# The first chunk of sequence 0 fetched on two hardware queues and cast on two engines, instead of one casting fetch on GpSimd's queue

## The chip, the cores and the metric

The kernel runs on one core of one Trainium2 chip. The metric is the device time of one execution in microseconds. Three timed runs of the kernel before gave 863.15, 863.33 and 863.42 us; the median is 863.33 us.

The core has a matrix engine (TensorE, "PE" in the profile, with "PEld" for its weight loads), VectorE ("DVE"), ScalarE ("ACT"), GpSimd ("POOL") and SyncE ("SP"), which here only issues transfers. Transfers are issued from three queues: GpSimd's (the profile's "software_dynamic" queue q0), SyncE's (hardware queue q1) and ScalarE's (hardware queue q10). All three feed the same 16 DMA engines.

## The reference, cut to what matters

```python
X = rfft(x, axis=1)                       # x: 8 sequences of 3008 rows of 256, fp32
y = irfft(X * (filt_r + 1j * filt_i)[None], n=3008, axis=1)
t = y.reshape(24064, 256)
xn = t / sqrt(mean(t * t, -1) + 1e-6) * rms_g
g, val = xn @ w_gate, xn @ w_val          # 256 -> 1536
out = (g * sigmoid(g) * val) @ w_out      # 1536 -> 256
```

A global filter mixes each sequence along its length, and a gated feed-forward block follows on all 24064 rows.

## The kernel before, in words

The transform of length 3008 = 47 x 64 is done as matmuls: a 64-point stage with the table `wa`, a 47-point stage with the tables `wb`, the filter, and the two stages back with `wi` and `wai`. Everything on TensorE is fp16 with fp32 accumulation, apart from a few fp32 transposes. The feed-forward block (`gv`, `down`) is the bulk of the work: 8 sequences x 6 tiles x 12 slices of the hidden size.

The mixing of sequences 1 to 7 is spread between the feed-forward slices of the sequences before them by a planner (`fit`, `at`), and the order of each engine's instructions is then fixed. Sequence 0 has nothing to hide behind: its mixing is a preface, written out by hand ahead of the main loop, in this order on TensorE:

- `fill(10)` (L643): ten matmuls of 512 columns on a zeroed tile whose result nobody reads; they need no transfer.
- `a0(0)` (L644), then `fill(4)`, `a0(1, 2)`, three small transposes (`psg`, L650 and L651), `fill(3)`, `a0(3)`, `fill(4)`, `a0(4, 5)`. One `a0(gq)` is two `a0_unit` calls (L353): eight matmuls of 128 columns in all (L357), which take four of the 24 columns of x as weights and `wa` as the moving operand; ScalarE and VectorE copy the two banks out (L195, L197).
- `f_unit` (L385, matmuls L389), which transposes the filter, alternating with `tr0_unit` (L362, transposes L367), then `b_unit`, `yt0_unit`, `bi_unit`, `first_norm` and the first `gv`.

x of one sequence comes in four chunks of six columns (`XC` = 6, `NXC` = 4). `x_load` (L174) fetches one with a single casting transfer on GpSimd's queue, fp32 in memory to fp16 in a tile of the pool `xp` (4 buffers). `a0(0)` reads columns 0 to 3, all in chunk 0; `a0(1)` reads 4 to 7, `a0(2)` 8 to 11, `a0(3)` 12 to 15, and `a0(4, 5)` 16 to 23, so that the last two need chunk 3.

On GpSimd's queue stand, in order: chunks 0 to 3 of x (L614, L186), the filter in six pieces of 512 KB (`f_load`, L382) with a part of `wb` before the sixth, the rest of `wb`, `wi`, and the feed-forward weights (`w_load`, L594). A transfer of this queue takes one of eight semaphores in turn, and the ninth waits until the first has landed, the tenth until the second, and so on; GpSimd's waits in its timeline show this. On SyncE's queue stand `tab` (L616: `wa`, `wai` and the identities, 160 KB) and three transfers of at most 1 KB into `tail` (L619, L620), which the transposes `psg` read.

The fp32 staging pool `stg` has four buffers, used in turn: the three pairs of filter pieces, then the feed-forward weights, then the tiles `y`.

The start of the preface, as it stands in the kernel before:

Of the kernel before, what the change touches and what calls it, by code (L numbers as in the profile page):

```python
# [10 lines left out]
FP32 = mybir.dt.float32  # L11
FP16 = mybir.dt.float16
# [5 lines left out]
N1 = 47  # L18
N2 = 64
NF = N // 2 + 1  # L20
P = 128
D = 256
# [3 lines left out]
H = 24  # L26
# [7 lines left out]
XC = 6  # L34
NXC = H // XC
# [66 lines left out]
def kernel(  # L102
# [11 lines left out]
    nc = tc.nc  # L114

    tab_np, wb_np, wi_np = _make_tables()
    tab_d = nc.inline_tensor(tab_np, name="tab_t").ap()
# [6 lines left out]
    stg = ctx.enter_context(tc.tile_pool(name="stg", bufs=4))  # L124
    xp = ctx.enter_context(tc.tile_pool(name="xp", bufs=4))
# [17 lines left out]
    tab = glob.tile([P, 5 * P], FP16)  # L143
# [20 lines left out]
    st = {b: {"x": {}, "t1": {}, "t2": {}, "s": {}, "yt": {}, "t4": {}, "y": {}, "sq": {},  # L164
              "u": {}, "xn": {}} for b in range(B)}

    def raw(src, row, ap):
        return bass.AP(tensor=src.tensor, offset=src.offset + row * D, ap=ap)
# [5 lines left out]
    def x_load(b, c):  # L174
        t = xp.tile([P, XC, D], FP16, tag="xc", name="xc")
        row = b * N + c * XC
        src = lambda n, w, lo=0: raw(x.flatten_outer_dims(), row + lo, [[N1 * D, n], [H * D, 2], [1, w * D]])
        if b == B - 1 and c == NXC - 1:
            w = XC - 1
            nc.vector.memset(t[96:P, w, :], 0.0)  # L180
            nc.gpsimd.dma_start(t[:, 0:w, :].rearrange("p a d -> p (a d)"), src(N2, w))
            nc.gpsimd.dma_start(t[0:P - 2, w, :], src(N2 - 1, 1, w))
            nc.gpsimd.dma_start(t[P - 2:P - 1, w, :],
                                raw(x.flatten_outer_dims(), row + w + (N2 - 1) * N1, [[D, 1], [1, D]]))
        else:
            nc.gpsimd.dma_start(t.rearrange("p a d -> p (a d)"), src(N2, XC))  # L186
        st[b]["x"][c] = t

    def bank(i, name):
        pool, tag = ((psM, "mx"), (psG, "pg"), (psV, "pv"), (psB, "mb"), (psO, "po0"))[i]  # L190
        return pool.tile([P, 512], FP32, tag=tag, name=name)

    def copy(eng, out, in_, scale=None):
        if eng == "A":
            nc.scalar.activation(out=out, in_=in_, func=AXT.Copy, **({} if scale is None else {"scale": scale}))  # L195
        elif scale is None:
            nc.vector.tensor_copy(out=out, in_=in_)  # L197
        else:
            nc.vector.tensor_scalar(out=out, in0=in_, scalar1=scale, scalar2=None, op0=ALU.mult)
# [223 lines left out]
    def fill(n, bk=0):  # L423
        ps = bank(bk, "pf")
        for _ in range(n):
            nc.tensor.matmul(ps, ss3[0][:, 0, 0, :], ss3[0].rearrange("p k e q -> p (k e q)")[:, 0:512], start=True, stop=True)
# [181 lines left out]
                                        op0=ALU.mult, op1=ALU.mult)  # L608

    with tc.manual_schedule():  # L610
        nc.vector.memset(ss3[0], 0.0)
        nc.vector.memset(epsb, 1e-6 * Y_SCALE * Y_SCALE)
        nc.scalar.activation(out=warm, in_=epsb.to_broadcast([P, 4]), func=AXT.Sqrt)
        for c in range(NXC):  # L614
            x_load(0, c)
        nc.sync.dma_start(tab, tab_d)  # L616
        tail = op.tile([P, 4, D], FP32, tag="o3", name="tail")
        for f, src in ((0, filt_i), (1, filt_r)):
            nc.sync.dma_start(tail[0:1, f, :], raw(src, NF - 1, [[D, 1], [1, D]]))  # L619
# [18 lines left out]
        def a0(*gqs):  # L638
            for gq in gqs:
                for dh in range(2):  # L640
                    a0_unit(gq, dh, E[dh], 1 + dh)

        fill(10)  # L643
        a0(0)  # L644
        fill(4)
        a0(1, 2)
# [32 lines left out]
        for p in range(UN + 3):  # L679
            if 3 <= p < UN:  # L680
                b_unit(0, od[p], (0, 3)[p % 2])
                s_part(0, od[p], 1)
            if p == 0:
                f_unit(2, 1, 1, "A")
                f_neg(4, 12, (1,))
                f_last()
                f_neg(0, 4)
                w_load(2)
                wo_load(0)
                f_neg(16, 16)  # L690
                wo_load(1)
                for c in range(3):
                    x_load(1, c)
                for q in range(3):
                    w_gain(q)
            if 2 <= p < UN + 1:
                yt0_unit(od[p - 2], "A", 1)
            if p == UN + 1:
                yt0_unit(UN - 1, "V", 1, slice(0, 2))
                yt0_unit(UN - 1, "A", 0, slice(2, 4))  # L700
            if 4 <= p < UN + 3:
                bi_unit(0, od[p - 4], "AV"[p == UN + 1], 2)
            if UN + 1 <= p < UN + 3:
                fill(1, 1)
# [8 lines left out]
        nc.gpsimd.tensor_copy(out=seen, in_=st[0]["t4"][1][:, 0, 0:4])  # L713
        wo_load(2)
        x_load(1, 3)
        first_norm()

# [92 lines left out]
        for b in range(1, B):  # L810
            t = (b - 1) * 72
# [73 lines left out]
```

## Time and profile before

| | |
|---|---|
| time, median of three runs | 863.33 us (863.15 to 863.42) |
| profiled execution, span from first to last instruction | 861.4 us |
| PE busy | 852.4 us, 99% of the span |
| ACT, DVE, POOL busy | 612.4, 557.2, 297.8 us |
| PE's share of the chain that ended last | 96% |
| first matmul of `a0(0)` | 6.06 us after the span's start |
| first matmul of `f_unit` | 13.03 us |

For the profiled execution the profile gives the span; the median of the timed runs is 1.9 us above it, and this part lies ahead of the first and behind the last instruction. PE is busy nearly all the time, and its busy time includes the matmuls of `fill`, which do no work of the reference. All that the change touches lies in the first 14 us, so the views to read are those of that stretch: the chain of waits, the timeline of PE, ACT and POOL, and the DMA packets of each queue in narrow windows. In a timeline, a row gives start, duration, engine, line, operation and count; the bracket at its end is the idle time just before it and what ended it. In a DMA window, a queue's row gives packets, MB, and the time that the packets took as a share of 16 engines.

### The profile page before, as it was taken

The numbers are of one execution on the slowest core, as the hardware profiler recorded it, in microseconds if no ns is written. First come the engines' busy times: TensorE is split into PE (matmuls) and PEld (weight loads), VectorE is DVE, ScalarE is ACT, GpSimd is POOL, SyncE is SP. The second block draws the span as 40 slices with busy tenths as digits, with TensorE's granted clock in tenths as the row PEclk, the third lists the DMA queues.
The fourth block names the chain that finished last, engine by engine and source line by source line (L and its number), as shares of the span: only waits on it lengthen the run. The fifth ranks groups of instructions, "written<-read, shape, count | busy, mean of one in ns | idle before, by whom it ended". The sixth has DMA issues, their size and how long they took to land.

```text
span 861.4 us, 17024 instructions
## 1 busy us (share of the span) xinstructions
PE 852.4 (99%) x6142; PEld 532.2 (62%) x6142; DVE 557.2 (65%) x926; ACT 612.4 (71%) x1339; POOL 297.8 (35%) x346
## 2 busy tenths in 40 slices
PE   8999999999999999999999999999999999999997
PEld 6755666566666666666666666666666666665664
DVE  5857655776666666666666676767666665555554
ACT  4986777787588756887577856888567765777443
POOL 5725742453144322534034430444123430132000
PEclk9999999999999999999999999999999999999999
DMA  9995778765975476656755548433564331521101
GB/s 283 270 204 124 150 164 168 139 130 121 197 137 129 121 150 111 151 107 147 139 127 113 132 98 180 108 87 101 131 127 93 97 70 42 124 54 49 62 25 50
DMA packets 198237, 107.98 MB, mean 125 GB/s; under 512 B 158566, under 2 KB 182520, under 8 KB 198152
## 3 DMA queue, kind: packets, MB, share of 16 engines
q1 hardware_dynamic: 189464, 85.52, 44.1%
q0 software_dynamic: 8544, 21.24, 12.7%
q8 instruction: 48, 0.79, 0.4%
q14 instruction: 37, 0.30, 0.1%
q10 hardware_dynamic: 144, 0.13, 0.0%
HBM read 45.78 MB, written 35.65 MB: 95 GB/s over the span
## 4 chain that ended last, share of the span: by engine, by line
PE 96%; DMA 1%; ACT 1%; DVE 1%; issue 0%; POOL 0%; POOLq 0%
PE po L563 28%; PE pg L546 28%; PE pv L546 28%; PE psb L241 3%; PE psi L285 3%; PE psn L314 2%; PE psa L206 2%; DMA fs<-in_filt_i_dram 1%; PE psy L418 1%; PE psf L389 1%; PE pst L367 0%; ACT sg L550 0%; POOL xc L186 0%; DVE s L231 0%; DVE hh L551 0%
## 5 line engine op out<-in xcount | busy, mean ns | idle before, releaser
L551 DVE TENSOR_TENSOR hh<-pv,sg 128x512 f16<-128x512 f32 (+2 forms) x578 | 391.5, 678 | 286.4 <-ACT sg L550 221.9
L550 ACT ACTIVATE sg<-pg 128x512 f16<-128x512 f32 (+2 forms) x578 | 337.4, 584 | 217.6 <-PE pg L546 213.4
L546 PE MATMUL pg<-xn,wg 128*128 128x512 f16 (+2 forms) x1156 | 338.1, 374 | 0.1
L546 PE MATMUL pv<-xn,wv 128*128 128x512 f16 (+2 forms) x1156 | 338.1, 374 | 0.0
L563 PE MATMUL po<-wo,hh 128*128 128x256 f16 x2256 | 332.7, 273 | 0.0
L563 PEld LDWEIGHTS <-hh 128*128 128x128 f16 x2256 | 213.4, 98 | 105.5 <-issue 0.6
L268 POOL TENSOR_TENSOR ss<-s,s 128x384 f16<-128x384 f16 x112 | 101.9, 911 | 273.2 <-DVE s L234 245.2
L546 PEld LDWEIGHTS <-wv 128*128 128x128 f16 x1156 | 112.9, 98 | 130.7
L546 PEld LDWEIGHTS <-wg 128*128 128x128 f16 x1156 | 111.4, 98 | 17.0 <-issue 0.3
L340 POOL TENSOR_TENSOR xt<-y,rho 128x1024 f16<-128x1024 f32 (+1 forms) x46 | 85.4, 1856 | 2.8
L322 ACT ACTIVATE junk<-y 128x256 f16<-128x256 f32 x180 | 74.3, 413 | 2.8
L231 DVE TENSOR_TENSOR s<-psb,ff 128x384 f16<-128x384 f32 x124 | 67.6, 547 | 0.7 <-ACT ff L195 0.6
L234 DVE TENSOR_TENSOR s<-psb,ff 128x384 f16<-128x384 f32 x124 | 67.6, 546 | 0.0
L195 ACT ACTIVATE uu<-psi 128x384 f16<-128x384 f32 (+1 forms) x127 | 61.6, 486 | 1.5 <-DMA out_dram<-o 0.5
L195 ACT ACTIVATE y<-psn 128x512 f32<-128x512 f32 (+1 forms) x95 | 55.7, 588 | 4.2
L285 PEld LDWEIGHTS <-yt 96*128 96x128 f16 x512 | 35.4, 97 | 26.7 <-issue 1.0
L332 POOL TENSOR_TENSOR rho<-u,mhalf 128x4 f32<-128x4 f32 (+1 forms) x46 | 46.5, 1010 | 3.8
L330 POOL TENSOR_SCALAR u<-ss 128x4 f32<-128x4 f32 (+1 forms) x46 | 8.9, 193 | 104.8 <-ACT junk L322 103.8
L195 ACT ACTIVATE t<-psa 128x512 f16<-128x512 f32 x70 | 41.4, 594 | 3.1 <-PE psa L206 1.7
L285 PE MATMUL psi<-wi,yt 96*128 96x96 f16 x512 | 42.9, 205 | 0.1
L241 PE MATMUL psb<-wb,t 96*128 96x96 f16 x480 | 40.1, 206 | 0.3 <-DVE s L234 0.2
L241 PEld LDWEIGHTS <-t 96*128 96x128 f16 x480 | 28.7, 97 | 12.8 <-DVE s L234 3.3
(101 smaller groups left out, 366.2 us busy)
## 6 DMA issues: line engine op xcount, KB each, us to landing
out_dram<-o SPq DMA_DIRECT2D x40, 512.0 KB, 3.6
xc<-in_x_dram POOLq DMA_DIRECT2D x31, 384.0 KB, 5.6
z_tmp<-t SPq DMA_DIRECT2D x28, 384.0 KB, 2.7
t<-z_tmp SPq DMA_DIRECT2D x28, 384.0 KB, 6.0
out_dram<-o SPq DMA_DIRECT2D x7, 384.0 KB, 2.7
fs<-in_filt_i_dram POOLq DMA_DIRECT2D x3, 512.0 KB, 10.8
fs<-in_filt_r_dram POOLq DMA_DIRECT2D x3, 512.0 KB, 11.2
ws<-in_moe_w_gate_dram POOLq DMA_DIRECT2D x3, 512.0 KB, 9.8
```

What stands on the lines that cost most here:

```text
L195: nc.scalar.activation(out=out, in_=in_, func=AXT.Copy, **({} if scale is None else {"scale": scale}))
L231: eng.tensor_tensor(out=o, in0=ps, in1=f1, op=ALU.mult)
L234: eng.tensor_tensor(out=o, in0=ps[:, :, ::-1, :], in1=f2, op=ALU.mult)
L241: nc.tensor.matmul(ps[:, ts(k, KR)], st[b]["t2"][kk // KC][:, kk % KC, ds(dh * P, P)], wb[0:KR, kk, :], start=True, stop=True)
L268: nc.gpsimd.tensor_tensor(out=ss3[g % 3][:, :, dh, 0:KR], in0=s[0], in1=s[1], op=ALU.add)
L285: nc.tensor.matmul(ps[:, k, :], yt[0:KR, k, dh, :], wi[0:KR, 4 * g + k, :], start=True, stop=True)
L322: nc.scalar.activation(out=junk, in_=y[:, i, ts(u, D)], func=AXT.Square, accum_out=ss[:, 2 * i + u:2 * i + u + 1])
L340: nc.gpsimd.tensor_tensor(out=xt[:, 0:n, :], in0=y.rearrange("p a (u d) -> p (a u) d", u=2)[:, 0:n, :], in1=rho[:, 0:n].unsqueeze(2).to_br ...
L546: nc.tensor.matmul(ps[:, 0:w], wt[:, dt_, ts(jt, P)], xn[:, q0:q1, dt_, :], start=(dt_ == 0), stop=(dt_ == 1))
L550: nc.scalar.activation(out=sg[:, c], in_=pg[:, 0:w], func=AXT.Silu)
L551: nc.vector.tensor_tensor(out=hh[:, c], in0=pv[:, 0:w], in1=sg[:, c], op=ALU.mult)
L563: nc.tensor.matmul(po[s4 // 2][:, s4 % 2, :], hh[:, ts(s4, P)], wo[:, jt, :], start=(jt == 0 and s4 % 2 == 0), stop=(jt == JT - 1 and (s4 ...
```

## The change

Chunk 0 of sequence 0 is no longer fetched by `x_load`. A new function fetches it as fp32, without a cast, into a buffer of the staging pool: columns 2 to 5 (512 KB) on ScalarE's queue, columns 0 and 1 (256 KB) on SyncE's queue. The transfer of `tab` is moved ahead of it, to the top, and stays the first on SyncE's queue; the transfers into `tail` follow behind columns 0 and 1. On ScalarE the issue stands ahead of the activation that loads the first table. GpSimd's queue begins with chunk 1. Ahead of `a0(0)`, ScalarE casts columns 0 and 1 and VectorE columns 2 to 5 into the fp16 tile that the matmuls read. `fill(10)` becomes `fill(7)`. Nothing is changed behind `a0(0)`; on every engine the order of the other instructions is the same.

```diff
+    X0 = 2
+
+    def x_first():
+        t = xp.tile([P, XC, D], FP16, tag="xc", name="xc")
+        raw_t = stg.tile([P, XC, D], FP32, tag="stg", name="xs")
+        for eng, lo, hi in ((nc.scalar, X0, XC), (nc.sync, 0, X0)):
+            eng.dma_start(raw_t[:, lo:hi, :].rearrange("p a d -> p (a d)"),
+                          raw(x.flatten_outer_dims(), lo, [[N1 * D, N2], [H * D, 2], [1, (hi - lo) * D]]))
+        st[0]["x"][0] = t
+        return t, raw_t
...
     with tc.manual_schedule():
+        nc.sync.dma_start(tab, tab_d)
+        xt0, xs0 = x_first()
         nc.vector.memset(ss3[0], 0.0)
         nc.vector.memset(epsb, 1e-6 * Y_SCALE * Y_SCALE)
         nc.scalar.activation(out=warm, in_=epsb.to_broadcast([P, 4]), func=AXT.Sqrt)
-        for c in range(NXC):
+        for c in range(1, NXC):
             x_load(0, c)
-        nc.sync.dma_start(tab, tab_d)
         tail = op.tile([P, 4, D], FP32, tag="o3", name="tail")
...
-        fill(10)
+        fill(7)
+        copy("A", xt0[:, 0:X0, :], xs0[:, 0:X0, :])
+        copy("V", xt0[:, X0:XC, :], xs0[:, X0:XC, :])
         a0(0)
         fill(4)
```

## The prediction

> **What bounds the kernel now.** I read the chain of waits first. The page gives PE 96% of it, so a change to the start moves the end by as much as it moves the moment from which PE runs without a gap. The chain over the first 15 us shows that moment:
>
> ```profile
> 0.63 0.63 issue
> 1.25 2.37 POOL xc L186 x4
> 3.63 9.27 DMA fs<-in_filt_i_dram
> 12.90 0.14 issue
> 13.03 1.06 PE psf L389 x8
> ```
>
> Until 13.03 us the chain is GpSimd's queue: four chunks of x, then the first filter piece, which lands at 12.90. From 13.03 to the first feed-forward matmul at 43.4 the chain has only PE, ACT and DVE pieces. So the first filter matmul is the milestone: what moves it moves the end one for one, and an earlier landing helps only if PE can use it. The timeline of PE shows how far it is from being late itself:
>
> ```profile
> 1.45 4.45 PE L426 MATMUL pf<-ss 128*128 128x512 f16 x10 [1.45 <-DVE epsb L612]
> 6.06 1.03 PE L357 MATMUL psa<-tab,xc 128*128 128x128 f16 x8 [0.17 <-DMA xc<-in_x_dram]
> 6.89 1.14 PE L426 MATMUL pf<-ss 128*128 128x512 f16 x4
> 7.86 1.06 PE L357 MATMUL psa<-tab,xc 128*128 128x128 f16 x16
> ...
> 11.22 0.28 PE L357 MATMUL psa<-tab,xc 128*128 128x128 f16 x2
> 11.68 0.96 PE L357 MATMUL psa<-tab,xc 128*128 128x128 f16 x14 [0.18 <-DMA xc<-in_x_dram]
> 13.03 0.74 PE L389 MATMUL psf<-tab,fs 128*128 128x128 f32 x5 [0.40 <-DMA fs<-in_filt_i_dram]
> ```
>
> Two things stand in it. Between 6.06 and 13.03 PE is nearly full: it waits for chunk 3 for some 0.35 us (11.33 to 11.68) and for the filter for 0.5. PE may thus start a0(0) at most 0.9 us later before it becomes the bound. And PE runs at half rate at first: the ten fills take 0.43 us each, the eight matmuls from 6.06 take 0.83/8 = 0.104 us, while the 16 from 7.86 to 8.75 take 0.056 each and later fills 0.216. The rate doubled about 7.1 us in, 5.6 us after the first matmul. (The granted clock reads 1.00 in these windows; I take the spacing.)
>
> **What the change removes.** GpSimd's queue loses chunk 0. Its timeline gives chunk landings from the waits that they end: 6.30, 8.16, 10.07, 11.91, so 1.85 us of transfer per chunk, and 1.28 us per filter piece (13.18 to 14.46). The 0.52 us of issue that goes hides nothing. The ninth transfer, which waited for chunk 0, now goes out at once; the others wait for the same transfers as before. Three fills go: 1.28 us of PE work that covered waiting, so nothing on the path; their cover for the half rate is costed below.
>
> **What it adds on the queues.** The two hardware pieces are 512 KB (one filter piece: 1.28 us of all 16 engines) and 256 KB (half: 0.64), so the data is 1.92 us instead of 1.85. The gain can only be in when it flows. tab was issued at 0.73 and its packets ran from 1.72 to 2.6; GpSimd's first transfer was issued at 1.25 and its packets began at 2.75. So the hardware pieces have about 1.0 us of free engines, of which tab needs 0.64 (its share of 1.7 to 2.7). After that they meet chunk 1. How the engines divide themselves decides the case. Two windows show it:
>
> ```profile
> q0 software_dynamic: 14, 0.04, 87.1%
> ```
>
> This is 2.85 to 3.60 us: the first software packets hold the engines for most of 0.75 us, and no hardware packet moves, though tail transfers issued up to 1.88 us are still due (five hardware packets follow in 3.6 to 4.3). And 51.5 to 54.3 us, a z_tmp store of 128 packets of 3072 B on SyncE's queue beside GpSimd's:
>
> ```profile
> q0 software_dynamic: 127, 0.34, 61.4%
> q1 hardware_dynamic: 133, 0.38, 36.7%
> ```
>
> The two queues go one packet for one. The store's packets needed 0.367 x 2.8 = 1.03 us of the engines and took 2.8. Per engine a store has 8 packets, and so have tab, each hardware piece and each chunk.
>
> So per engine: a software packet is 1.85/8 = 0.23 us, a 4 KB one 0.16, a 2 KB one 0.08, a tab one 0.055. By 2.75, less a start of 0.2, some four tab packets and four of ScalarE's piece are done. Then 0.85 us of the first software packet, to 3.6; four rounds of tab, ScalarE's piece and software, 4 x (0.055 + 0.16 + 0.23) = 1.8, to 5.4; then SyncE's piece, queued behind tab, eight rounds of (0.08 + 0.23) = 2.5, to 7.9. With 0.1 for the landing, columns 0 and 1 are there at 8.0. Lower bound: hardware first, tab + 1.92 = 2.56 us from 1.72, and the 0.3 us by which tab landed after its last packet: 4.6. Upper: completion packets take turns too, 0.5 more: 8.5. I take 8.0, since both rows show alternation.
>
> For GpSimd's queue, chunk 1 takes chunk 0's place behind the same first packet, with 1.7 us of hardware work left in its way: chunk 3 and the filter land only 0.2 to 0.4 us earlier (with hardware first, up to 1.2).
>
> **The casts.** ScalarE's (512 elements): between 0.41 (256 elements with a sum, L322) and 0.60 (512 elements); I take 0.59, plus 0.1 of hand-over, on the path. VectorE's (1024 elements): 0.69 (1024 fp16, L197) to 1.2 (twice the 512-element 0.69, less one start); its data comes at 5.5, so it ends by 6.8, under ScalarE's. If SyncE's piece came first, VectorE's would set the time, 0.1 to 0.6 more. Behind the waiting casts only the copies of a0 are queued, which need them anyway. The issue ahead of ScalarE's table load (0.36 to 0.66 us) delays a load that ended at 2.0 and that nobody needs before the cast. The tail transfers behind SyncE's piece are used 2.8 us after a0(0) starts: hidden. The staging buffer must be free before a weight transfer at 15.7: hidden. So a0(0) starts at 8.0 + 0.7 = 8.7 instead of 6.06.
>
> **PE from there.** The chain in PE's order from a0(0) to the last of a0(5) at full rate: 0.45 + 0.86 + 0.89 + 0.50 + 0.65 + 0.45 + 0.86 + 0.89 = 5.55 us (windows of PE's timeline; before: 6.06 to 12.47 with 0.35 of waiting and 0.5 of half rate). At half rate each stretch doubles. Seven fills end at 1.45 + 7 x 0.43 = 4.45, and PE then stands for over 4 us. Bounds for the half rate behind a0(0): none (the rate is kept through the gap), to 6.8 us. The one row is 5.6 us from a first matmul with one 0.35 us pause; I take 4, since the weight of it is unknown, which costs 2.0. The first filter matmul then comes at 8.7 + 5.55 + 2.0 + 0.05 = 16.3 instead of 13.03: 3.3 us later. By then the filter has long landed. Nothing gives the time back: from there the chain has no DMA piece. **The sum** is 863.33 + 3.3 = 866.6 us; made against the profiled execution it is a span of 861.4 + 3.3 = 864.7, with the same 1.9 around it.
>
> Two rules of the Trainium skill are weighed here. The Trainium skill, TensorE: Matmul & The Clock Gate, "What's actually happening", says that the array is at half clock until one fixed window of about 3.4 us was busy, and again after an idle one; the 5.6 us here agree. By it seven fills (3.0 us) are too short, the half rate would last an estimated 2.5 to 6 us behind a0(0), and the sum would be 866 to 868.
> The Trainium skill, DMA: Bandwidth & Descriptors, "Queues, rings and completion order", says that an engine drains a packet of some 9 to 17 descriptors from one queue before it turns to the next; the 127 against 133 above do not show that. By it the eight descriptors of a piece would go in one turn, which is the second rival.
>
> **Rivals.**
> 1. Late data, but the half rate ends soon or the alternation is milder: a0(0) at 7.0 to 7.5, half rate for 1 to 3 us: milestone at 13.1 to 14.6, 863.4 to 864.9. For it: the 0.85 us of the first software packet need not repeat behind hardware traffic. Against: no hardware packet between 2.85 and 3.60.
> 2. The other side: a hardware piece goes through in one turn. Then columns 0 and 1 land at 4.6 to 5.0, VectorE's cast ends by 5.6, PE stands for about 1 us, its half rate ends within some 2 us, and its chain would be done at 5.6 + 5.55 + 1.0 = 12.15, so the filter decides: 0.6 to 1.2 us earlier, 862.4. It decides if a0(0) starts before 6.5. For it: idle engines before 2.75 and between 2.85 and 3.6. Against: the 127 and 133.
> 3. More than 0.2% faster would need the filter to land 1.7 us earlier; the engines are busy 0.99 and more from 4.0 us on, so all of the idle time before would have to be filled.
>
> **How the numbers follow.** 0.2% of 863.33 is 1.73 us, about what a measurement can tell from no change. Forecast (a0(0) after 7.8, half rate again): 0.62, range 864.9 to 868.0. Rival 1: 0.18, of which 0.03 is above 865.06. Rival 2: 0.16. Rival 3: 0.04. So slower 0.65, same 0.31, faster 0.04. For 8 in 10 the range is 862.8 to 867.9: it takes in most of rival 2 and drops the ends.
>
> **What would show it.** Right: a0(0) waits until 8 to 9 us and is released by ScalarE's cast, which waits for SyncE's piece; fills behind a0(0) at 0.43 us; the first filter matmul at 15 to 17.5 with no DMA wait; all later stages shifted by the same amount. Wrong: hardware packets in one burst before 4.5 us, fills at 0.216 us right behind a0(0), or a filter matmul that still waits for its transfer.

## The result and the profile after

The changed kernel takes 867.15 us (median of four runs, 866.71 to 868.0) against 863.24 us for the kernel before (four runs, 863.15 to 863.42): a ratio of 1.0046 with a 95% interval of 1.0032 to 1.006. It is slower by 3.9 us. The forecast was 866.6, slower by 3.3.

The profiled execution of the changed kernel took 867.2 us, with a span of 865.4 against 861.4. The first lines of its page:

```profile
span 865.4 us, 17023 instructions
PE 852.3 (98%) x6139; PEld 532.8 (62%) x6139; DVE 558.5 (65%) x927; ACT 613.1 (71%) x1340; POOL 297.5 (34%) x345
```

PE's busy time is what it was (852.4 before), since the three fills that are gone are made up for by matmuls that run longer at half rate. The span is 4.05 us longer (865.43 against 861.38), and by so much more PE stands. The chain of waits over the first 18 us shows most of it (start, duration, what):

```profile
0.73 0.35 SPq L622
1.09 0.06 issue
1.15 7.19 DMA xs<-in_x_dram
8.34 0.02 issue
8.36 0.64 ACT xc L206
9.00 0.05 issue
9.04 1.03 PE psa L368 x8
...
15.64 0.89 PE psa L368 x16
16.53 0.02 issue
16.55 1.14 PE psf L400 x8
```

The chain that ran through GpSimd's queue and the filter now runs through SyncE's piece of chunk 0, issued at 1.15 and landed 7.19 us later, then ScalarE's cast, then PE alone. The first filter matmul comes at 16.55 instead of 13.03. The timeline of PE has the rate at which it went there:

```profile
1.45 3.17 PE L437 MATMUL pf<-ss 128*128 128x512 f16 x7 [1.45 <-DVE epsb L625]
9.04 1.03 PE L368 MATMUL psa<-tab,xc 128*128 128x128 f16 x8 [4.42 <-ACT xc L206]
9.87 1.91 PE L437 MATMUL pf<-ss 128*128 128x512 f16 x4
11.58 1.60 PE L368 MATMUL psa<-tab,xc 128*128 128x128 f16 x16
...
14.61 1.03 PE L437 MATMUL pf<-ss 128*128 128x512 f16 x4
15.47 1.06 PE L368 MATMUL psa<-tab,xc 128*128 128x128 f16 x16
16.55 1.14 PE L400 MATMUL psf<-tab,fs 128*128 128x128 f32 x8
```

The seven fills stand 0.43 us apart to their end, so PE has not reached its full rate when they are over; then it stands for 4.42 us. The four fills behind `a0(0)` take 1.91 us, the four from 14.61 take 1.03: by their starts 0.43 us each against 0.216. The rate doubles within the 16 matmuls from 11.58, at about 12.7, so the half rate lasted 3.7 us behind `a0(0)`. No bracket names a DMA from 9.04 on. From there nothing is given back: the first gate matmul of the feed-forward block moves from 43.38 to 46.93, and all 578 gate activations from 44 us to the end stand 3.55 to 3.56 us later than in the trace of before.

One part of the difference does not lie at the start. The last store of each kernel, in SyncE's timeline, of before:

```profile
857.64 0.56 SPq L578 DMA_DIRECT2D out_dram<-o  x1
```

and of after:

```profile
861.23 0.54 SPq L589 DMA_DIRECT2D out_dram<-o  x1
```

From its start to the end of the span are 861.38 - 857.64 = 3.74 us before and 865.43 - 861.23 = 4.20 us after. So 0.46 us are lost behind the last store, which the change doesn't touch. The last store itself is 861.23 - 857.64 = 3.59 us later, nearly all of it from the start (3.52 at the first filter matmul), and 3.59 + 0.46 make the 4.05 by which the span grew.

GpSimd's waits show that its own queue, relieved of chunk 0, became later and not earlier:

```profile
8.79 0.55 POOL L635 DMA_DIRECT2D wb<-wb_t  x1 [2.50 <-DMA xc<-in_x_dram]
10.50 0.53 POOL L393 DMA_DIRECT2D fs<-in_filt_r_dram  x1 [1.16 <-DMA xc<-in_x_dram]
12.34 0.54 POOL L637 DMA_DIRECT2D wb<-wb_t  x1 [1.31 <-DMA xc<-in_x_dram]
13.64 0.54 POOL L638 DMA_DIRECT2D wb<-wb_t  x1 [0.76 <-DMA fs<-in_filt_i_dram]
```

These end with the landings of chunks 1, 2, 3 and the first filter piece; before, the same waits ended at 8.16, 10.07, 11.91 and 13.18. The queue is 0.4 to 0.6 us late throughout, without a consequence, since PE reaches the filter only at 16.55.

The DMA packets of each queue (packets, MB, share of 16 engines) from 2.75 to 4.25 us:

```profile
q10 hardware_dynamic: 107, 0.39, 71.6%
q1 hardware_dynamic: 27, 0.06, 10.8%
```

and from 5.5 to 8.0 us:

```profile
q0 software_dynamic: 173, 0.49, 101.2%
q1 hardware_dynamic: 29, 0.04, 4.7%
```

In the first there is no packet of GpSimd's queue (q0) at all, although its first transfer was issued at 1.26 and the engines were 18% idle. ScalarE's piece landed at 5.42. Of SyncE's, 111 of the 128 packets had started by 5.5 as well; 17 are among the 29 of the second window, the rest there being `tail`'s and a few of 4 B. But these 17 run beside GpSimd's queue, the last starts at 7.7, and a transfer has landed when its last packet has. The trace has 16 completion records of this piece, read here as one for each engine: thirteen stand by 6.06, the last three at 6.94, 7.86 and 8.34. So a few engines make the piece late.

### The profile page after: what moved, and what is told of

Read it like the earlier page. It is cut to its first block, busy times and chain, and to the rows that moved or that the text cites. A ratio compares the mean times of both kernels' runs of the same rounds, so it can differ in the third digit from the quotient of the medians.

```text
span 865.4 us, 17023 instructions
## 1 busy us (share of the span) xinstructions
PE 852.3 (98%) x6139; PEld 532.8 (62%) x6139; DVE 558.5 (65%) x927; ACT 613.1 (71%) x1340; POOL 297.5 (34%) x345
## 4 chain that ended last, share of the span: by engine, by line
PE 96%; ACT 1%; DVE 1%; DMA 1%; issue 0%; SPq 0%
PE po L574 28%; PE pg L557 28%; PE pv L557 28%; PE psb L252 3%; PE psi L296 2%; PE psn L325 2%; PE psa L217 2%; DMA xs<-in_x_dram 1%; PE psy L429 1%; PE psf L400 1%; PE pf L437 0%; PE psa L368 0%; PE pst L378 0%; DVE s L242 0%; DVE hh L562 0%
```

## The experiments

Each is made on the changed kernel unless it says otherwise, and its ratio is to the kernel before on the same chip, whose medians were 863.16 to 863.37 us. A hardware transfer is one on SyncE's or ScalarE's queue. What the forecast rested on comes first: the half rate, then the landing, then the queue of GpSimd, and last the part at the end that no step had foreseen.

### The half rate of PE

**Sixteen fills instead of seven**, so that PE works until shortly before the data:

```diff
-        fill(7)
+        fill(16)
```

> The changed kernel with 16 fills ahead of a0(0) instead of 7, nothing else. They last from 1.45 to at most 1.45 + 16 x 0.43 = 8.3 us, less if the rate doubles on the way, so they end before columns 0 and 1 are there (cast ended at 9.0). Theory (the seven fills leave PE standing for 4.4 us, and the half rate of the 3.66 us behind a0(0) costs half of that): a0(0) still at about 9.0, the fills behind it at 0.216 us, the first filter matmul at 14.7 instead of 16.55, time 867.15 - 1.85 = 865.3 us. Rival (the late data is all of it, the rate comes back by itself): filter matmul at 16.5, 867.1 us.

Measured: 865.39 us (eight runs, 863.47 to 865.73), ratio 1.0023 (1.0013 to 1.0034). The timeline of PE in this kernel:

```profile
1.45 6.31 PE L437 MATMUL pf<-ss 128*128 128x512 f16 x16 [1.45 <-DVE epsb L625]
9.12 0.62 PE L368 MATMUL psa<-tab,xc 128*128 128x128 f16 x8 [1.37 <-ACT xc L206]
9.58 1.03 PE L437 MATMUL pf<-ss 128*128 128x512 f16 x4
...
14.88 1.14 PE L400 MATMUL psf<-tab,fs 128*128 128x128 f32 x8
```

The data comes no earlier (`a0(0)` at 9.12), yet the fills behind it run at 0.216 us and the first filter matmul comes at 14.88. From `a0(0)` to it are 5.76 us, against 7.51 in the changed kernel: the half rate is worth 1.75 us, shown by taking it away alone. Here the rate had doubled at about 6.9 us, within the sixteen fills, and a pause of 1.37 us did not bring the half rate back. In the changed kernel it had not doubled before the pause, so that kernel does not show what its 4.42 us of standing do by themselves: seven fills are too few to reach the full rate.

**The kernel before with seven fills**, the smallest part of the change done alone:

```diff
-        fill(10)
+        fill(7)
```

> The kernel before with 7 fills instead of 10, nothing else: chunk 0 comes on GpSimd's queue as before. Theory (half rate after a pause): a0(0) stays at 6.06, PE stands from 4.6 to 6.06, the half rate then lasts 2.5 to 6 us behind a0(0), PE's chain ends at 6.06 + 5.6 + 1.3 to 3.0 = 13.0 to 14.7, so the filter matmul comes 0 to 1.6 us later: 863.2 to 864.9 us, and more scatter between executions than before. Rival (the number of fills is indifferent as long as the data is the bound): 863.2 us, filter matmul at 13.03.

Measured: 864.09 us (ten runs, 863.34 to 864.34), ratio 1.0009 (1.0 to 1.0019). Chunk 0 comes on GpSimd's queue as before, 0.25 us later in the profiled execution. Its timeline of PE:

```profile
6.31 1.03 PE L357 MATMUL psa<-tab,xc 128*128 128x128 f16 x8 [1.69 <-DMA xc<-in_x_dram]
7.14 1.91 PE L426 MATMUL pf<-ss 128*128 128x512 f16 x4
...
14.13 1.15 PE L389 MATMUL psf<-tab,fs 128*128 128x128 f32 x8
```

With a pause of only 1.69 us, `a0(0)` and the fills behind it run at half rate as in the changed kernel, and the first filter matmul comes 1.1 us late, of which 0.25 is the landing. So dropping three fills costs some 0.9 us even with no late data. The sum had called the fills "nothing on the path" but for the half rate, which is what shows here.

### The landing of SyncE's piece

**GpSimd's queue held back until chunk 0 is there**, by two tiny copies on GpSimd that read both pieces ahead of its first transfer:

```diff
+        for c in (0, X0):
+            nc.gpsimd.tensor_copy(out=seen, in_=xs0[:, c, 0:4])
         for c in range(1, NXC):
             x_load(0, c)
```

> The changed kernel with two small copies on GpSimd ahead of chunk 1, which read chunk 0's two hardware pieces, so that no software transfer is under way while they land. Theory (SyncE's piece was late because it shared the engines with GpSimd's queue): it lands at about 4.8 us instead of 8.34, VectorE's cast and ScalarE's end by 5.9, a0(0) at about 5.9. Rival (it is late by its own place: behind tab on SyncE's queue, 2 KB packets, beside ScalarE's piece): it lands at 7 to 8 us still. Either way GpSimd's queue begins 4 us later, the first filter piece lands at about 15 to 17 us and is then the bound: 865.5 to 867.5 us.

Measured: 867.43 us (one run). Its DMA issues (columns: size, us from issue to landing) and the timeline of ACT and PE:

```profile
xs<-in_x_dram SPq DMA_DIRECT2D x1, 256.0 KB, 4.2
```

```profile
5.42 0.63 ACT L206 ACTIVATE xc<-xs 128x512 f16<-128x512 f32 x1 [2.50 <-DMA xs<-in_x_dram]
6.11 1.03 PE L368 MATMUL psa<-tab,xc 128*128 128x128 f16 x8 [1.49 <-ACT xc L206]
...
10.77 0.96 PE L368 MATMUL psa<-tab,xc 128*128 128x128 f16 x14 [1.71 <-DMA xc<-in_x_dram]
...
13.79 1.91 PE L437 MATMUL pf<-ss 128*128 128x512 f16 x4
```

Without GpSimd's packets SyncE's piece lands at 5.40 instead of 8.34. So 2.9 us of its 7.19 are what GpSimd's queue costs it; the theory is right, its 4.8 was too early by 0.6. The kernel gains nothing, since GpSimd's first issue then stands at 6.09, chunk 1 lands at 10.72, and some 1.7 us after the wait for it PE falls back from full rate to half rate (four fills in 1.91 us at 13.79). This is one execution.

**One transfer for all six columns on ScalarE's queue**, first with seven fills, then with ten:

```diff
-        for eng, lo, hi in ((nc.scalar, X0, XC), (nc.sync, 0, X0)):
+        for eng, lo, hi in ((nc.scalar, 0, XC),):
```

> The changed kernel with all six columns of chunk 0 in one transfer of 768 KB on ScalarE's queue; the casts are unchanged. ScalarE's piece of 512 KB landed at 5.42 us with packets at about 0.16 us each per engine. Theory (SyncE's piece is late because it stood second on its queue, so that on some engines it met software packets one for one): one transfer that starts at 2.0 lands at 6.0 to 6.7, a0(0) at 6.8 to 7.5, filter matmul at 14.0 to 15.0 (half rate as in the changed kernel), 864.7 to 865.6 us. Rival (any 768 KB of hardware transfer ends on the same slow engine at about 8.3): a0(0) at 9.0, 867.1 us.

> All of chunk 0 in one transfer on ScalarE's queue, as in the run before it, with 10 fills instead of 7. There a0(0) came at 6.24 us, the rate doubled at 9.0, the filter piece landed at 12.74 and PE's chain ended at 13.33. Theory (what was left of the loss is the half rate behind seven fills): the fills end at 5.73, PE pauses half a microsecond, the rate doubles at 5 to 8.3, PE's chain would end by 12.1 to 13.0, so the filter's landing decides: first filter matmul at 12.9, 863.17 - 0.15 = 863.0 us, within 0.1% of the kernel before, and little scatter. Rival (a cost of the new fetch that is not seen yet): 863.6 us, as with seven fills.

Measured: 863.63 us with seven fills (ten runs, 862.44 to 864.02; ratio 1.0002, 0.9993 to 1.0012), and 862.78 with ten (eleven runs, 862.31 to 863.14; ratio 0.9994, 0.9985 to 1.0003). With seven, the 768 KB are issued at 0.73 and land at 5.54, earlier than all that was expected: three times the data of SyncE's piece, on one hardware queue, is there 2.8 us before it. With ten fills the timeline of PE has

```profile
12.55 1.06 PE L400 MATMUL psf<-tab,fs 128*128 128x128 f32 x8 [0.39 <-DMA fs<-in_filt_i_dram]
```

and the filter is the bound again, landed at 12.42 instead of 12.90. This is the lowest median of all, 0.4 us under the kernel before, which eleven runs can't tell from no change.

**Both pieces on ScalarE's queue**, to see if SyncE's queue is to blame:

```diff
-        for eng, lo, hi in ((nc.scalar, X0, XC), (nc.sync, 0, X0)):
+        for eng, lo, hi in ((nc.scalar, X0, XC), (nc.scalar, 0, X0)):
```

> The changed kernel with both pieces on ScalarE's queue, still as two transfers, columns 2 to 5 first; tab alone on SyncE's; 7 fills. Tells whether two transfers or the second queue made columns 0 and 1 late. Theory (it is the second piece that meets software packets one for one on an engine that is behind, on whichever queue it stands): the second piece lands at 6.5 to 8.3, a0(0) at 7.2 to 9.0, 865 to 867 us. Rival (SyncE's queue, behind tab and sharing turns with ScalarE's, made it late): as with one transfer on ScalarE's queue, lands at 5.6, a0(0) at 6.3, 863.7 us.

Measured: 868.56 us (four runs, 868.06 to 868.85), ratio 1.006 (1.0046 to 1.0073), the slowest of all. Its DMA issues:

```profile
xs<-in_x_dram ACTq DMA_DIRECT2D x1, 512.0 KB, 4.2
...
xs<-in_x_dram ACTq DMA_DIRECT2D x1, 256.0 KB, 7.7
```

Issued at 0.73 and 1.40, they land at 4.94 and 9.14. So neither SyncE's queue nor the transfer of `tab` ahead is needed to make a piece late. As in the changed kernel, though, the late piece is the second transfer of its queue.

**Halves by partition**, 64 partitions each, so that both pieces have 64 packets of 6144 B and equal size:

```diff
-        for eng, lo, hi in ((nc.scalar, X0, XC), (nc.sync, 0, X0)):
-            eng.dma_start(raw_t[:, lo:hi, :]...,
+        for eng, h in ((nc.scalar, 0), (nc.sync, 1)):
+            eng.dma_start(raw_t[h * 64:h * 64 + 64]...,
```

> The changed kernel with chunk 0 split by partitions instead of columns: partitions 0 to 63 (384 KB, packets of 6144 B) on ScalarE's queue, 64 to 127 on SyncE's queue behind tab; same bytes, same two queues, 7 fills. In the changed kernel each engine has 8 packets of 4096 B and 8 of 2048 B, here 8 of 6144 B in all, as in the single transfer that landed at 5.54. Theory (what counts is how many hardware packets still wait on the slowest engine when the software packets come, as each then waits for one of them): both halves land at 5.5 to 6.0 us, a0(0) at 6.3 to 6.8, 863.6 to 864.5 us. Rival (two hardware transfers on two queues make an engine late whatever the packets): the later half lands at about 8.3, 867 us.

Measured: 867.63 us (four runs, 867.13 to 868.24), ratio 1.005 (1.0034 to 1.0067). ScalarE's half, issued at 0.73, lands at 5.23; SyncE's, issued at 1.15, at 7.66, against 5.5 to 6.0 expected. So the number of packets alone doesn't set it; again the piece issued second is the late one. `a0(0)` starts at 8.43, 0.6 us earlier than in the changed kernel, and the time is no shorter: the half rate lasts longer here, and from `a0(0)` to the first filter matmul (16.76) are 8.33 us instead of 7.51.

**All on SyncE's queue, behind `tab`**, and then **the same with `tab` on ScalarE's queue**, so that chunk 0 is SyncE's first issue. The two differ in nothing but this second edit:

```diff
-        for eng, lo, hi in ((nc.scalar, X0, XC), (nc.sync, 0, X0)):
+        for eng, lo, hi in ((nc.sync, 0, XC),):
...
-        nc.sync.dma_start(tab, tab_d)
+        nc.scalar.dma_start(tab, tab_d)
```

> The changed kernel with all of chunk 0 in one transfer on SyncE's queue, behind tab; nothing on ScalarE's queue; 7 fills. Theory (one transfer of few large packets is what lands early, not the queue): it starts 0.3 to 0.5 us later than on ScalarE's queue, lands at 5.8 to 6.4 us, a0(0) at 6.5 to 7.1, 863.8 to 864.8 us. Rival (the place behind tab on SyncE's queue made columns 0 and 1 late): it lands at 8 or later, 867 us or more.

> The run with all of chunk 0 on SyncE's queue, with one thing exchanged: tab goes to ScalarE's queue, so that chunk 0's transfer is the first on SyncE's queue and is issued at 0.73 us instead of 1.16; 7 fills. Theory (a hardware transfer that is issued at 0.73 is through before the software packets move, one that is issued at 1.15 or later goes with them one for one, whichever queue it is on): it lands at 5.5 us, hardly any software packet moves before 4.3, a0(0) at 6.3, 863.6 us. Rival (SyncE's queue takes turns with GpSimd's and ScalarE's does not): it lands at 7.5 to 8.4 as before, a0(0) at 8.3 to 9.1, 867 us.

Measured: 867.55 us with `tab` ahead (four runs, 866.8 to 867.82; ratio 1.0048, 1.0033 to 1.0063), 863.52 with chunk 0 first (ten runs, 862.47 to 864.2; ratio 1.0001, 0.9991 to 1.001). The packets of the first, from 4 to 6 us:

```profile
q1 hardware_dynamic: 65, 0.40, 51.9%
q0 software_dynamic: 62, 0.19, 47.9%
```

and of the second, its only queue with packets from 2.75 to 4.25 us:

```profile
q1 hardware_dynamic: 76, 0.47, 84.6%
```

Issued at 1.16, the 768 KB take turns with GpSimd's queue one packet for one and land at 8.37; the first of their 16 completion records stands at 6.63. Issued at 0.73 they run alone, and land at 5.44. The same transfer on the same queue, 0.43 us earlier, is there 2.9 us earlier. Over all the runs:

| issued at | piece | landed at |
|---|---|---|
| 0.73 | 384 to 768 KB, ScalarE's or SyncE's queue | 4.89 to 5.55 |
| 1.15 to 1.40 | 256 to 768 KB, ScalarE's or SyncE's queue | 7.66 to 9.14 |
| 1.15, GpSimd's queue held back | 256 KB | 5.40 |

In all these kernels but the last, GpSimd's first transfer is issued at about 1.25. What separates the first two rows is the time of issue, or the place on the queue: each piece of the first row is the first transfer of its queue, each of the second stands behind another one (`tab`, or ScalarE's first piece). No run here parts the two, and why either decides it the traces don't show. Neither is enough by itself: in the last row a piece issued at 1.15 behind `tab` is in time once GpSimd's queue is held back.

### What GpSimd's queue gains

**A third of chunk 0 on hardware**, columns 0 and 1 on ScalarE's queue from the start, columns 2 to 5 back on GpSimd's queue as a casting transfer, ten fills:

```diff
-        for eng, lo, hi in ((nc.scalar, X0, XC), (nc.sync, 0, X0)):
+        for eng, lo, hi in ((nc.scalar, 0, X0),):
...
+        nc.gpsimd.dma_start(t[:, X0:XC, :]..., raw(x.flatten_outer_dims(), X0, ...))
...
-        fill(7)
+        fill(10)
...
-        copy("V", xt0[:, X0:XC, :], xs0[:, X0:XC, :])
```

> Columns 0 and 1 of chunk 0 as 256 KB on ScalarE's queue, cast by ScalarE; columns 2 to 5 by a casting transfer on GpSimd's queue, ahead of chunk 1; 10 fills. Theory (the hardware piece uses the engines between 2.3 and 3.6 us, in which the first software packets of the kernel before moved little, and as it is small the software queue starts no later for it): GpSimd's queue is 0.6 us shorter (a third of 1.85), the filter piece lands at 12.3, a0(0) at 5.7 to 6.0, first filter matmul at 12.4 to 12.6, 862.6 to 862.8 us, faster than both kernels. Rival (software packets start only when the hardware piece is through, as they did at 4.3 us beside the larger pieces): the filter lands at 12.7 to 12.9, 863.0 to 863.2 us.

Measured: 864.46 us (eleven runs, 863.33 to 865.05), ratio 1.0012 (1.0003 to 1.0021). Both expectations missed. The hardware piece lands at 3.81 and the rest of chunk 0 at 6.16, but chunk 1 only at 9.71 and the filter at 14.67, and PE waits for each:

```profile
9.76 0.96 PE L370 MATMUL psa<-tab,xc 128*128 128x128 f16 x14 [2.06 <-DMA xc<-in_x_dram]
...
14.81 1.06 PE L402 MATMUL psf<-tab,fs 128*128 128x128 f32 x8 [0.44 <-DMA fs<-in_filt_i_dram]
```

**The kernel before with half of the first filter piece on hardware**, 256 KB on ScalarE's queue from the start, the other half left on GpSimd's, x as before:

```diff
+        if (i, f) == (0, 0):
+            lo = FR4 // 2
+        nc.gpsimd.dma_start(t[:, f, lo:FR4]..., raw(src, row + lo, ...))
...
+        fst[0] = stg.tile([P, 2, FR4, D], FP32, tag="stg", name="fs")
+        nc.scalar.dma_start(fst[0][:, 0, 0:FR4 // 2]..., raw(filt_i, 0, [[FR4 * D, P], [1, FR4 // 2 * D]]))
```

> The kernel before (chunk 0 by GpSimd, 10 fills) with half of the first filter piece, 256 KB that need no cast, on ScalarE's queue from the start and the other half on GpSimd's. Theory (engines that were idle before 3.6 us carry it): chunks land as before, at most 0.2 us later, the filter's rest lands 0.6 earlier at 12.3, PE's chain of a0 then ends last at 12.5, first filter matmul at 12.6, 862.75 us. Rival (the hardware piece holds the software queue back by its own 0.64 us): chunks 0.6 later, filter unchanged at 12.9, a0(0) at 6.6, 863.2 us or a little more.

Measured: 865.41 us (eleven runs, 863.24 to 866.78), ratio 1.0022 (1.0013 to 1.0031). Missed again. The piece is in by 4.19, yet chunk 0, on GpSimd's queue, lands at 8.67 instead of 6.02:

```profile
8.72 1.03 PE L357 MATMUL psa<-tab,xc 128*128 128x128 f16 x8 [3.05 <-DMA xc<-in_x_dram]
```

In both profiled executions, a quarter of a megabyte of hardware traffic that is over by 3.8 to 4.2 us costs GpSimd's queue 1.8 to 2.6 us, although it takes bytes off that queue. It is a few engines again: of the 16 completion records of the late chunk fourteen stand by 8.28 in the first and by 6.40 in the second, the last two at 8.66 and 9.71, and at 7.80 and 8.67. What holds these engines is not settled, and the spread of the times (3.5 us in the last) suggests that it differs from one execution to the next.

### The end of the program

From the last store's issue to the end of the span are 3.59 to 3.74 us in the kernel before and in all experiments with one hardware transfer more or none, and 4.19 to 4.21 in the changed kernel and the four experiments with two more. If the hardware transfers take eight semaphores in turn, as those of GpSimd's queue do, two more give the last store another one. **Six more transfers of 1 KB** on SyncE's queue, into an unused part of `tail`, make the count eight more and bring the turn back:

```diff
+        for j in range(6):
+            nc.sync.dma_start(tail[2 * j:2 * j + 2, 3, 0:P], moe_rms_g.rearrange("(a p) -> a p", p=P))
```

> The changed kernel with six more transfers of 1 KB on SyncE's queue behind the tail transfers, into a part of that tile that nobody reads: eight hardware transfers more than the kernel before instead of two. Hardware transfers take eight semaphores in turn. In the kernel before 3.74 us lie between the issue of the last store and the end of the span, in the changed kernel 4.20, and in every run with two transfers more than before 4.2, with none or one more 3.6 to 3.7. Theory (at the end SyncE waits for the semaphores in a fixed order, and with two more the last store has the first of them, so that the others are gone through after it): with eight more the turn is where it was, 3.7 us, and the time is 0.45 us below the changed kernel's where the start is the same. Rival (each further transfer costs): 4.2 us or more. The start is as in the changed kernel, a0(0) at 8.5 to 9.5 us.

Measured: 866.54 us (seven runs, 865.8 to 867.31), ratio 1.0037 (1.0024 to 1.0049), with a span of 864.0. The last store in SyncE's timeline:

```profile
860.50 0.54 SPq L589 DMA_DIRECT2D out_dram<-o  x1
```

The tail is 864.0 - 860.5 = 3.5 us, as short as before although six transfers were added. So the number alone doesn't set it, and the turn of eight fits; SyncE's waits show that two of the six new transfers wait for the landings of chunk 0's two pieces (3.2 us in all), as the tenth and eleventh hardware transfers must if each waits for the one eight places before it. That the place in the turn costs the 0.46 us rests on this one count. How much of the 0.6 us between the medians comes from this can't be said, since `a0(0)` happened to start at 8.44 in this execution (SyncE's piece landed at 7.73).

## Why the prediction was right

**The milestone.** "What moves it moves the end one for one": 3.52 us at the first filter matmul, 3.55 at the first gate matmul, 3.55 to 3.56 at every gate activation behind. Right. Over the profiled executions of all fourteen kernels the time less the milestone is 849.9 to 851.0 us, whatever moved it, and the higher values belong to the kernels with two more hardware transfers.

**`a0(0)` released by ScalarE's cast, which waits for SyncE's piece.** Right, at 9.04 (8.7 forecast). The landing, 8.34 against 8.0, is the difference; the cast took 0.63 and its hand-over 0.07 (0.59 and 0.1 forecast). VectorE's cast, 5.44 to 6.20, took 0.76 and is hidden, as forecast with data at 5.5 (5.42).

**How the engines divide themselves.** The landing came out, the working did not. The sum let "0.85 us of the first software packet" hold the engines to 3.6, and then counted rounds of `tab`, ScalarE's piece and GpSimd's queue. In the trace GpSimd's queue moves nothing before 4.4; ScalarE's piece has by 4.25 started all but 8 of its 128 packets, ahead of all. One-for-one turns with GpSimd's queue show in the run with all of chunk 0 on SyncE's queue behind `tab` (65 against 62 packets), and holding that queue back brings SyncE's piece in 2.9 us earlier, so the wait on which the forecast is built is there. But most of the piece (111 of 128 packets) had started by 5.5, where the sum has it only begin at 5.4, and what came after 6.06 was the work of three engines. With the first 3 us wrong, a landing within 0.4 us of the forecast is partly luck. The Trainium skill, DMA: Bandwidth & Descriptors, "Queues, rings and completion order", has an engine drain some 9 to 17 descriptors of one queue before it turns to the next: the 65 against 62 don't agree with that for this pair of queues, nor does the first completion at 6.63; the run with chunk 0 first on SyncE's queue, where no packet of GpSimd's moves before 4.65, could be read so.

**GpSimd's queue.** "Chunk 3 and the filter land only 0.2 to 0.4 us earlier" is the step that failed: they landed 0.43 and 0.46 later. The bytes taken off the queue are not what sets it; 256 KB of hardware traffic ahead of it cost it 1.8 to 2.6 us in two experiments. In the three kernels with all of chunk 0 in one early transfer the filter landed at 12.42 to 12.74, 0.2 to 0.5 us earlier than in the kernel before. It had no consequence for the result, since the filter was no longer awaited.

**The half rate.** "I take 4 ... which costs 2.0": it lasted 3.7 us and from `a0(0)` to the first filter matmul PE took 7.51 us, 1.96 more than the 5.55 at full rate. Sixteen fills give 1.75 of that back. The term is right: seven fills do not reach the full rate, and the half rate goes on behind the data. That 4 us were so near is partly luck, as one row stood behind it. In the eight other kernels in which PE came to `a0(0)` at half rate after a pause and then waited for no data before the filter, the stretch from `a0(0)` to the first filter matmul took 7.09 to 8.33 us, 1.5 to 2.8 more than at full rate. The cost of three fills, "nothing on the path" apart from this, is the 0.9 us of the kernel before with seven. The Trainium skill, TensorE: Matmul & The Clock Gate, "What's actually happening", lets the rate go by fixed windows of about 3.4 us; the estimate of 2.5 to 6 us that the prediction worked out from it holds the 3.7. The full idle window that it asks for before the half rate comes back is not met in the run with GpSimd's queue held back: its fills at 13.79 are at half rate, its 14 matmuls from 10.77 (0.06 us each) at full rate, and PE had stood for only 1.71 us ahead of those.

**The term that was missing.** The 0.46 us behind the last store. Nothing in the sum looked at the end of the program. With the 3.59 us up to that store it makes the 4.05 us of span, where the sum had 3.3.

**The rivals.** The first is out by `a0(0)` at 9.04 and the milestone at 16.55, the third, which needs a faster kernel, by the slower one. The second rival's time, 862.4, which needs chunk 0 by 5.0, is about what one early transfer with ten fills reaches (862.78, chunk 0 in for `a0(0)` at 6.26). So a hardware transfer that goes ahead of GpSimd's queue does exist; this change misses it with its second piece, which is issued 0.42 us after the first and stands behind `tab`. With seven fills even that is not enough: `a0(0)` then came at 6.14 and 6.24, before the rival's bound of 6.5, but the first filter matmul at 13.92 and 13.33, as the half rate cost 2.2 and 1.5 us and not the 1.0 of its sum. No version found is told apart from the kernel before as faster: from there on the filter, on GpSimd's queue, decides again.

## What to carry to other kernels

A fetch split over two queues is as late as the later piece's slowest engine: before splitting, ask when each piece is issued, behind what it stands on its queue, and what else has been issued by then, since here one transfer of 768 KB issued first at 0.73 us landed 2.8 us before the 256 KB issued second at 1.15. Where PE waits for the first data, fill matmuls up to that moment are worth their place: stopping them at 4.5 us, before the rate had doubled, cost 1.75 us more behind the wait. Where two nearly equal kernels differ by half a microsecond, look behind the last store too.

## What was not expected of the hardware

- GpSimd's queue, issued at 1.25 us, moved no packet before 4.4 us in the changed kernel and before 4.59 in those with one early transfer of 768 KB, though the engines were 14 to 18% idle from 2.75 to 4.25. With sixteen fills, which change nothing at this point, its first packet came at 3.97. With 256 KB alone, columns 0 and 1 on ScalarE's queue, 72 of its packets moved in that window beside 105 hardware packets. In the kernel before its packets began at 2.75.
- 256 KB of hardware traffic over by 3.8 to 4.2 us left GpSimd's queue 1.8 to 2.6 us late afterwards, by the last two of 16 completion records. The cause stays open.
- Two more hardware transfers at the start lengthened the end of the program by 0.46 us, eight more did not (3.74, 4.20 and 3.5 us behind the last store's issue).
- The half rate does not need a long pause: one of 1.71 us after 3 us of work brought it back, with a delay of some 1.7 us behind the pause, while one of 1.37 us after 6.3 us of work did not.
